# A new order for the front of a long fused kernel (results, scores, updates, x and loads), and a set place for three merges

## The chip, the core and the metric

The kernel runs on one core of one Trainium2 chip. The metric is device time in microseconds (us): the median of three runs of the kernel before is compared with that of the kernel after. A profile of one execution shows what each engine did: TensorE (PE, with its weight loads PEld), VectorE (DVE), ScalarE (ACT), GpSimd (POOL) and SyncE (SP), which issues nearly all the transfers (DMA).

## What is computed

The reference, cut to its core (float32 in and out; 2 sequences of 768 rows, 8 heads of 64, 512 dimensions):

```python
# 1. attention with decay, in blocks of 64 with a running state
intra = einsum('bhij,bhjd->bhid', einsum('bhic,bhjc->bhij', qb, kb) * Dmask, vb)
out   = intra + einsum('bhid,bhde->bhie', qb * lam_pow, kv_state)
kv_state = lam_block * kv_state + einsum('bhsd,bhse->bhde', kb * rev_pow, vb)
# 2. a token MLP and a channel MLP (1536 hidden)
h = relu(xt @ w_tok1) @ w_tok2        # xt = x transposed, 768 -> 256 -> 768
u = x + h.T
x = u + relu(u @ w_ch1) @ w_ch2
# 3. Fourier mixing, a norm, a channel MLP (2048 hidden)
u  = x + real(fft(fft(x, axis=1), axis=2))
un = (u - mean) / sqrt(var + 1e-6)
return u + relu(un @ m_ch1) @ m_ch2
```

## The kernel before

All products run on TensorE in float32r. Where float32 accuracy is wanted, each operand is a rounded part (hi) and the rest (lo), and `mm3` (L142 to L146) issues three matmuls. `split` (L136) makes the two parts of an activation: ScalarE writes hi, VectorE lo. Weights come from HBM as 8-byte words and go through a conveyor (`convert`, L291): a load by SyncE into one of three `raw` buffers, two ScalarE instructions (L233, L235), two VectorE **merges** of the words (L254, L255), then hi on ScalarE (L283) and lo on GpSimd (L284). A `raw` buffer is free for the next load when the merges have read it. Weights are named by their use: `t1` and `t2` of the token MLP, (a, 0, f) and (b, 0, f) of the first channel MLP, (a, 1, f) and (b, 1, f) of the second.

**Order of work.** TensorE and SyncE run in the order in which the program emits their instructions. The order on ScalarE, VectorE and GpSimd is made by a planner when the kernel is compiled; each engine then works through its list in order. `tc.issue_after(ins)` puts the instructions of its block behind `ins` in the list of the engine that they share.

**The front.** Attention has 8 steps n (2 sequences times 4 pairs of heads). The string `EARLY` gives the order as words: `l` loads a step (keys, queries, then keys and values; 384, 384 and 768 KB), `s` is scores (L410, then four VectorE multiplications L413), `u` is the update of the state (ScalarE first scales the keys, L432; L438; a chain of VectorE steps, L442 and L444), `r` is the result (L460 on scores, L466 on states; two ScalarE copies, L468). `x` transposes a half of one sequence and splits it (L483), `h` and `o` are the two products of the token MLP (`h00`: sequence 0, first half of the hidden units), `m` is one step of the channel MLP, `c` one turn of the conveyor, `d` the same without a load, `w` keeps TensorE busy with transposes, and `k` loads a constant. Loads 0 to 3 and the three of `t1` are issued before the string. A step's q, k, v lie in one of five `half` buffers, which the tiles of `x` and later ones use too.

**Later.** `run` takes the channel MLPs unit by unit; `WHEN` gives, for each of 25 Fourier and norm pieces of a sequence, the half step at which it is emitted. Piece 18 in the list was `fourier_columns(b, 2)` and piece 19 `norm(b, (0, 1, 2, 3))`. In `norm`, the VectorE instructions L950 write the normalized rows (`unf`), which TensorE transposes in `norm_out` (L959). The last part runs in units of seven products (`seven`), with three PSUM accumulators (pa, pb, pc) in two banks; VectorE reads them (L660 to L680) and so frees the banks.

Of the kernel before, what the change touches and what calls it, by code (L numbers as in the profile page):

```python
# [16 lines left out]
ALU = mybir.AluOpType  # L17
# [12 lines left out]
HS = S // 2  # L30
NQ = 256
# [2 lines left out]
BIG = 12 * NQ  # L34


EARLY = """s0 w u0 w s1 r0 u1 s2 u2 l4 r1 s3 u3 c r2 s4 l5 r3 u4 d d x00 s5 d l6 u5 r4 s6 x01 h00 c r5 c h01 l7 u6 s7 u7 r6 o00
r7 m o01 x10 m x11 m h10 m h11 m m o10 o11 k"""

WHEN = ((67, 71, 77, 73, 74, 77, 75, 77, 77, 79, 80, 81, 85, 83, 86, 85, 87, 84, 88, 90, 92, 91, 94, 97, 98),  # L40
        (92, 92, 93, 95, 97, 98, 100, 100, 103, 106, 106, 108, 108, 108, 112, 110, 113, 115, 116, 116, 119, 117,
         118, 120, 123))

# [19 lines left out]
def body(ctx: ExitStack, tc: tile.TileContext, qkv, kT, lam, w_tok1, w_tok2,  # L63
# [15 lines left out]
    tt = nc.vector.tensor_tensor  # L79
# [16 lines left out]
    on_act = {("table", 0): table_load}  # L96
    on_dve = {}

    chain = {("t1", 0): 3, ("t1", 1): 3, ("t1", 2): ("st", 5)}

# [116 lines left out]
    def stage_abs():  # L219

        if at_["abs"] >= at_["load"]:
            return
        job = jobs[at_["abs"]]
        kind, key = job
        at_["abs"] += 1
        if kind in ("single", "sums"):
            return
        m = raw_p.tile([P, 512], U32, tag="man", name="m_" + "_".join(map(str, key)), bufs=BUFS["man"])[:, :width(key)]
        mans[job] = m
        late = {("t1", 2): ("out", 2), ("b", 0, 1): ("out", 6), ("b", 0, 3): ("hid", 1), ("a", 0, 4): ("hid", 1)}  # L230
        with tc.issue_after(lag.get("act", on_act[late.get(key, ("keys", 3))])), behind_urgent():
            lo, hi = words(job)
            nc.scalar.activation(f32(m), f32(hi), AF.Copy, scale=DOWN)  # L233
            halves = raws[job].bitcast(U16)[:, :4 * width(key)].rearrange("p (n t) -> p n t", t=4)
            nc.scalar.activation(lo, halves[:, :, 1], AF.Identity, scale=2.0 ** -13, bias=floor_by)  # L235
# [187 lines left out]
    def attention_states(b, hp, dT, pw):  # L423

        n = f"{b}_{hp}"
        t, sts = pair[b, hp]
        kn, v = (t[:, i, :].rearrange("p (c j) -> p c j", j=C) for i in (1, 2))
        m = NP * b + hp
        behind = (("table", 0), ("keys", 0), ("out", 0), ("out", 1), ("out", 2), ("x", 0), ("out", m - 2))[min(m, 6)]
        with tc.issue_after(on_act[behind]):  # L430
            for a in range(2):
                on_act["keys", NP * b + hp] = nc.scalar.activation(  # L432
                    kn[:, :NC - 1, a * D:(a + 1) * D], kn[:, :NC - 1, a * D:(a + 1) * D], AF.Copy,
                    scale=dT[:, 2 * hp + a, C - 1:C]).ins
        ups = acc_bank(f"u_{n}")
        for c in range(NC - 1):
            for a in range(2):
                nc.tensor.matmul(ups[a * D:(a + 1) * D, c * D:(c + 1) * D], kn[:, c, a * D:(a + 1) * D],  # L438
                                 v[:, c, a * D:(a + 1) * D], start=True, stop=True)
        state = temp((NC - 1) * D, f"state_{n}").rearrange("p (c e) -> p c e", c=NC - 1)  # L440
        up = ups[:, :(NC - 1) * D].rearrange("p (c e) -> p c e", c=NC - 1)
        nc.vector.tensor_copy(state[:, 0], up[:, 0])  # L442
        for c in range(1, NC - 1):
            chained = stt(out=state[:, c], in0=state[:, c - 1], scalar=pw[:, hp, C - 1:C], in1=up[:, c],  # L444
                          op0=ALU.mult, op1=ALU.add).ins
        on_dve[NP * b + hp] = chained
        pair[b, hp] = t, sts, state
# [28 lines left out]
    def token_in(b, half):  # L476

        xt = half_tile([P, 3, 2, DM], f"x_{b}_{half}", F32R)
        for i in range(3):
            c = 3 * half + i  # L480
            px = (acc_bank if b == 0 else ph_bank if i == 2 else x_bank)(f"px_{b}_{c}")
            for hp in range(NP):
                nc.tensor.transpose(px[:, hp * P:(hp + 1) * P], xT[b][:, hp, c * P:(c + 1) * P], ident)  # L483
            with tc.issue_after(on_dve[4]) if b == half == 0 else ExitStack():
                split(px, xt[:, i, 0, :], xt[:, i, 1, :])
            xs[b, c] = xt[:, i]
        if b == half == 0:
            on_act["x", 0], on_dve["x", 0] = on_act["split"], on_dve["split"]

    def token_hidden(b, t):  # L490
        ps = (acc_bank, x_bank)[b](f"h1_{b}_{t}")
# [11 lines left out]
    def token_out(b, c):  # L503
        t = half_tile([P, 4, 2, HS], f"uh_{b}_{c}", F32R)
        uh[b, c] = t
        for dt in range(4):
            ps = (acc_bank, x_bank)[b](f"ht_{b}_{c}_{dt}")
            ds = slice(dt * P, (dt + 1) * P)
            for k in range(2):
                need(("t2", k, c))  # L510
                w = wt_tiles["t2", k, c]
                mm3(ps[:, :HS], (h1[b, k][0][:, ds], h1[b, k][1][:, ds]), (w[:, 0, :HS], w[:, 1, :HS]), k == 0, k == 1)
            u = xT[b][:, dt, c * HS:(c + 1) * HS]
            tt(out=u, in0=ps[:, :HS], in1=u, op=ALU.add)
            if dt:
                split(*todo_split)
            todo_split = u, t[:, dt, 0, :], t[:, dt, 1, :]
        split(*todo_split)
        if b == 1:
            live.difference_update([("t2", k, c) for k in range(2)])  # L520
# [117 lines left out]
    def hidden(n, src):  # L638
        t = hid_p.tile([P, 2, HS], F32R, tag="hid", name=n)
        relu_split(src, t[:, 0, :], t[:, 1, :])  # L640
        return t

    def seven(b, p, between):

        n = f"{b}_{p}"
        f = 2 * p
        for key in (("a", 1, f), ("a", 1, f + 1), ("s", 1, p)):
            need(key)
        wa, wb = wt_tiles["a", 1, f], wt_tiles["a", 1, f + 1]
        sums = {k: (wt_tiles["s", 1, p][i], 256 * j) for k, (i, j) in SUMS.items()}  # L650
        x0, x1 = unh[b, 0], unh[b, 1]
        ts_ = {j: tops[b, j] for j in range(1, 5)}
        pa = ph_bank(f"pa_{n}")
        product(pa, (wa, 0), x0[:, 0:2], True)
        m1 = temp(HS, f"m1_{n}")
        nc.scalar.activation(m1, pa[:, :HS], AF.Copy)
        pb = ph_bank(f"pb_{n}")
        product(pb, sums["S2"], ts_[2], True)
        u2 = temp(HS, f"u2_{n}")
        tt(out=u2, in0=pb[:, :HS], in1=m1, op=ALU.add)  # L660
        between()
        product(pa, (wa, 256), x0[:, 2:4], False)
        hid[1, b, 0, f] = hidden(f"hid_{n}_11", pa[:, :HS])
        if "next" in lag:
            lag["act"] = lag["next"]
        lag["next"] = urgent["act"]
        product(pb, sums["S3"], ts_[3], False)
        v3 = temp(HS, f"v3_{n}")
        tt(out=v3, in0=pb[:, :HS], in1=m1, op=ALU.add)
        between()  # L670
        pc = ph_bank(f"pc_{n}")
        product(pc, sums["S1"], ts_[1], True)
        tt(out=v3, in0=pc[:, :HS], in1=v3, op=ALU.add)
        hid[1, b, 1, f + 1] = hidden(f"hid_{n}_22", v3)
        product(pb, (wb, 256), ts_[4], False)
        tt(out=m1, in0=pb[:, :HS], in1=m1, op=ALU.add)
        hid[1, b, 0, f + 1] = hidden(f"hid_{n}_21", m1)
        between()
        product(pc, sums["S4"], x1[:, 2:4], False)
        tt(out=u2, in0=pc[:, :HS], in1=u2, op=ALU.add)  # L680
        hid[1, b, 1, f] = hidden(f"hid_{n}_12", u2)
        for key in (("a", 1, f), ("a", 1, f + 1), ("s", 1, p)):
            used(key)
        between()
# [188 lines left out]
    def fourier_columns(b, T):  # L873
# [24 lines left out]
        z = temp(2 * (NQ + 1), f"z_{b}_{T}")  # L898
        zs[b, T] = [z[:, i * (NQ + 1):(i + 1) * (NQ + 1)] for i in range(2)]
        for i, op in enumerate((ALU.subtract, ALU.add)):  # L900
            tt(out=sides(zs[b, T][i])[1], in0=at[:, :NQ].rearrange("p (h j) -> p h j", h=2),
               in1=ps[1][:, :NQ].rearrange("p (h j) -> p h j", h=2), op=op)
        ends = z.rearrange("p (i n) -> p i n", i=2)[:, :, 0:P + 1:P]
        nc.scalar.activation(ends, at[:, 0:NQ + 1:NQ].rearrange("p (o c) -> p o c", o=1).to_broadcast([P, 2, 2]),
                             AF.Copy)
# [22 lines left out]
    def norm(b, rows):  # L928
# [18 lines left out]
        convert(1, ops)  # L947
        for i, r in enumerate(rows):
            un = temp(DM, f"unf_{b}_{r}")
            ts(out=un, in0=u3[b][:, r, :], scalar1=mv[:, i, 0:1], scalar2=rs[:, i:i + 1],  # L950
               op0=ALU.subtract, op1=ALU.mult)
            uns[b, r] = un

    def norm_out(b, rows):
# [41 lines left out]
    for b in range(B):  # L996
        for h, (fn, *args) in zip(WHEN[b], (
# [1 line left out]
                (fourier_ab, b, 1, 0), (fourier_ab, b, 1, 1), (fourier_d, b, 1, 0), (fourier_d, b, 1, 1),  # L999
                (fourier_sums, b, 0), (fourier_sums, b, 1), (fourier_y, b, 0), (fourier_y, b, 1),  # L1000
                (fourier_gather, b), (fourier_columns, b, 0), (fourier_rows, b, 0), (fourier_columns, b, 1),
                (fourier_rows, b, 1), (fourier_mid, b), (fourier_columns, b, 2), (norm, b, (0, 1, 2, 3)),
                (fourier_rows, b, 2), (norm_out, b, (0, 1)), (norm_out, b, (2, 3)), (norm, b, (4, 5)),
                (norm_out, b, (4, 5)))):
            side.setdefault(h, []).append((fn, args))
# [207 lines left out]
```

## Time and profile before

| | before |
|---|---|
| median of 3 runs | 600.46 us (599.66 to 601.36) |
| the profiled execution's own time | 599.12 us |
| its span, first to last instruction | 597.3 us |
| TensorE busy | 584.4 us, 98% of the span |
| VectorE busy | 403.6 us, 68% |
| ScalarE busy | 264.4 us, 44% |
| GpSimd busy | 134.0 us, 22% |
| mean granted TensorE clock | 0.997 of full speed |

TensorE is busy nearly all the time, so a change to the order can only win what TensorE still waits. Its 12.9 us of idle time are the room there is, with a short stretch in which its clock was at half. Matmuls overlap in the profile and their ends are modelled, so an idle time in brackets is somewhat shorter than the delay in the starts.

### The profile page before, as it was taken

Reading aid. Unit: us, or ns where it says so; the run is one execution under the profiler, and the core shown is the slowest. Engines: PE = TensorE matmul, PEld = TensorE weight load, DVE = VectorE, ACT = ScalarE, POOL = GpSimd, SP = SyncE. Lnnn points to the kernel's source line nnn. Section 1 sums busy time; section 2 is a strip of 40 time slices with the busy share of each in tenths; the row PEclk is TensorE's granted clock in tenths of the full one; section 3 lists DMA queues with packets and bytes.
Section 4 is the critical chain, followed back from the end, with each engine's and each line's share of the span. In section 5 each row is a group of like instructions: output and inputs, shape, how many; then the busy total and the mean of one; then the engine's idle time right before and its main releaser. Section 6 shows DMA issues by size and latency. Waiting matters only on the chain.

```text
span 597.3 us, 9553 instructions
## 1 busy us (share of the span) xinstructions
PE 584.4 (98%) x3704; PEld 546.0 (91%) x3704; DVE 403.6 (68%) x765; ACT 264.4 (44%) x511; POOL 134.0 (22%) x114
## 2 busy tenths in 40 slices
PE   8899999999999999999999999999999999999997
PEld 7787899999999999999999999899889998899985
DVE  6787982565585656858787896867785864654435
ACT  1566871355565555535364451334433444331110
POOL 4254340022240051001452110014401223220000
PEclk9899999999999999999999999999999999999999
DMA  7975440033548756510232001002421232200005
GB/s 272 396 281 208 148 156 21 1 105 107 160 173 248 270 171 195 165 47 1 72 89 71 19 1 36 19 19 70 142 88 36 89 123 89 88 2 1 0 1 211
DMA packets 24637, 65.58 MB, mean 110 GB/s; under 512 B 2824, under 2 KB 3984, under 8 KB 24592
## 3 DMA queue, kind: packets, MB, share of 16 engines
q1 hardware_dynamic: 24304, 64.83, 32.5%
q8 instruction: 29, 0.48, 0.3%
q10 hardware_dynamic: 288, 0.14, 0.1%
q14 instruction: 16, 0.13, 0.1%
HBM read 54.99 MB, written 9.97 MB: 109 GB/s over the span
## 4 chain that ended last, share of the span: by engine, by line
PE 84%; DMA 6%; DVE 6%; ACT 2%; issue 1%; POOL 1%; SPq 0%; DVEq 0%; POOLq 0%; ACTq 0%
PE ac L145 12%; PE ac L146 12%; PE ac L144 12%; PE ph L144 8%; PE ph L146 8%; PE ph L145 8%; DMA qkv<-qkv 3%; DMA raw_t_0d<-w_tok 2%; PE pb L146 2%; PE pb L145 2%; PE pb L144 2%; PE pa L144 1%; PE pc L146 1%; PE pa L146 1%; PE pc L144 1%; PE pc L145 1%
## 5 line engine op out<-in xcount | busy, mean ns | idle before, releaser
L524 DVE SCALAR_TENSOR_TENSOR hid<-ph,hid 128x384 fp32r<-128x384 f32 x68 | 37.6, 554 | 60.5 <-ACT hid L523 60.5
L146 PE MATMUL ac<-w_b,hid 128*128 128x512 f32 x192 | 75.8, 395 | 0.0
L145 PE MATMUL ac<-w_b,hid 128*128 128x512 f32 x192 | 75.7, 394 | 0.0
L144 PE MATMUL ac<-w_b,hid 128*128 128x512 f32 x192 | 75.0, 391 | 0.0
L144 PE MATMUL ph<-uh,w_a 128*128 128x384 f32 x192 | 64.7, 337 | 0.0
L144 PE MATMUL ac<-hid,w_b 128*128 128x384 f32 x192 | 64.5, 336 | 0.0
L523 ACT ACTIVATE hid<-ph 128x384 fp32r<-128x384 f32 x68 | 33.1, 487 | 70.6 <-PE ph L146 70.3
L145 PE MATMUL ac<-hid,w_b 128*128 128x384 f32 x192 | 64.3, 335 | 0.0
L146 PE MATMUL ph<-uh,w_a 128*128 128x384 f32 x192 | 64.3, 335 | 0.0
L145 PE MATMUL ph<-uh,w_a 128*128 128x384 f32 x192 | 64.3, 335 | 0.0
L146 PE MATMUL ac<-hid,w_b 128*128 128x384 f32 x192 | 64.2, 335 | 0.0
L284 POOL TENSOR_TENSOR w_a<-m_a,w_a 128x512 fp32r<-128x512 f32 x18 | 25.6, 1422 | 131.4 <-ACT w_a L283 131.4
L146 PEld LDWEIGHTS ac<-w_b,hid 128*128 128x128 f32 x192 | 36.0, 188 | 7.7
L145 PEld LDWEIGHTS ac<-w_b,hid 128*128 128x128 f32 x192 | 36.1, 188 | 6.0
L144 PEld LDWEIGHTS ac<-w_b,hid 128*128 128x128 f32 x192 | 36.1, 188 | 5.8
L284 POOL TENSOR_TENSOR w_b<-m_b,w_b 128x512 fp32r<-128x512 f32 x18 | 26.0, 1445 | 46.5 <-ACT w_b L283 32.4
L144 PEld LDWEIGHTS ph<-uh,w_a 128*128 128x128 f32 x192 | 36.1, 188 | 0.2 <-ACT uh L138 0.2
L145 PEld LDWEIGHTS ac<-hid,w_b 128*128 128x128 f32 x192 | 36.1, 188 | 0.2 <-DVE hid L524 0.2
L145 PEld LDWEIGHTS ph<-uh,w_a 128*128 128x128 f32 x192 | 36.1, 188 | 0.1
L144 PEld LDWEIGHTS ac<-hid,w_b 128*128 128x128 f32 x192 | 36.1, 188 | 0.0
L146 PEld LDWEIGHTS ph<-uh,w_a 128*128 128x128 f32 x192 | 36.0, 188 | 0.0
L146 PEld LDWEIGHTS ac<-hid,w_b 128*128 128x128 f32 x192 | 36.0, 188 | 0.0
(504 smaller groups left out, 1429.1 us busy)
## 6 DMA issues: line engine op xcount, KB each, us to landing
qkv<-qkv SPq DMA_DIRECT2D x7, 768.0 KB, 10.1
single_scratch<-m_a SPq DMA_DIRECT2D x16, 256.0 KB, 4.3
qkv<-qkv SPq DMA_DIRECT2D x10, 384.0 KB, 6.1
kp<-kT SPq DMA_DIRECT2D x8, 384.0 KB, 6.9
out<-u SPq DMA_DIRECT2D x11, 256.0 KB, 2.0
single_scratch<-m_b SPq DMA_DIRECT2D x10, 256.0 KB, 5.3
raw_t_0d<-w_tok SPq DMA_DIRECT2D x2, 384.0 KB, 11.6
raw_t_1d<-w_tok SPq DMA_DIRECT2D x2, 384.0 KB, 3.0
```

The lines of the kernel that those rows point to most:

```text
L144: nc.tensor.matmul(ps, wt[0], xt[0], start=first, stop=False, **kw)
L145: nc.tensor.matmul(ps, wt[0], xt[1], start=False, stop=False, **kw)
L146: nc.tensor.matmul(ps, wt[1], xt[0], start=False, stop=last, **kw)
L284: nc.gpsimd.tensor_tensor(out=t[:, 1, :n], in0=src, in1=f32(t[:, 0, :n]), op=ALU.subtract)
L523: mark("act", nc.scalar.activation(hi, ps, AF.Relu))
L524: mark("dve", stt(out=lo, in0=ps, scalar=0.0, in1=f32(hi), op0=ALU.max, op1=ALU.subtract))
```

## The change

The front's words get another order: `r1` goes ahead of `u2`, `r3` ahead of `s4`, `r4` ahead of `u5`, `x01` ahead of `s6`, and the load of step 7 right behind that of step 6, ahead of the loads of `t2`. Some VectorE merges and ScalarE conversions of weights get another place behind which they are put: those of (t1, 2) behind the state of step 5 and the result of step 3, the conversion of (t2, 0, 0) behind the split of `x01`, the merges of (a, 0, 1) behind the second addition of `o00`, and those of (a, 1, 10) behind the end of the first unit of seven. In sequence 1 the norm is emitted ahead of the third columns, whose VectorE subtraction and addition go behind the second row of `unf`. For sequence 0 the two swapped times in `WHEN` keep the order as it was.

```diff
-EARLY = """s0 w u0 w s1 r0 u1 s2 u2 l4 r1 s3 u3 c r2 s4 l5 r3 u4 d d x00 s5 d l6 u5 r4 s6 x01 h00 c r5 c h01 l7 u6 s7 u7 r6 o00
+EARLY = """s0 w u0 w s1 r0 u1 s2 r1 u2 l4 s3 u3 c r2 l5 r3 s4 u4 d d x00 s5 l6 l7 r4 u5 d x01 s6 h00 c r5 c h01 u6 s7 u7 r6 o00
 r7 m o01 x10 m x11 m h10 m h11 m m o10 o11 k"""
-WHEN = ((67, 71, 77, 73, 74, 77, 75, 77, 77, 79, 80, 81, 85, 83, 86, 85, 87, 84, 88, 90, 92, 91, 94, 97, 98),
+WHEN = ((67, 71, 77, 73, 74, 77, 75, 77, 77, 79, 80, 81, 85, 83, 86, 85, 87, 84, 90, 88, 92, 91, 94, 97, 98),
...
-    chain = {("t1", 0): 3, ("t1", 1): 3, ("t1", 2): ("st", 5)}
+    chain = {("a", 1, 10): "unit", ("t1", 0): 3, ("t1", 1): 3, ("t1", 2): 5, ("a", 0, 1): ("ht", 1)}
...
-        late = {("t1", 2): ("out", 2), ("b", 0, 1): ("out", 6), ("b", 0, 3): ("hid", 1), ("a", 0, 4): ("hid", 1)}
+        late = {("t1", 2): ("out", 3), ("t2", 0, 0): ("x", 1), ("b", 0, 1): ("out", 6), ("b", 0, 3): ("hid", 1), ("a", 0, 4): ("hid", 1)}
...
-        behind = (("table", 0), ("keys", 0), ("out", 0), ("out", 1), ("out", 2), ("x", 0), ("out", m - 2))[min(m, 6)]
+        behind = (("table", 0), ("keys", 0), ("out", 0), ("out", 1), ("out", 3), ("x", 0), ("out", m - 2))[min(m, 6)]
...
-        if b == half == 0:
-            on_act["x", 0], on_dve["x", 0] = on_act["split"], on_dve["split"]
+        if b == 0:
+            on_act["x", half] = on_act["split"]
...
-            tt(out=u, in0=ps[:, :HS], in1=u, op=ALU.add)
+            added = tt(out=u, in0=ps[:, :HS], in1=u, op=ALU.add).ins
+            if b == c == 0:
+                on_dve["ht", dt] = added
...
         hid[1, b, 1, f] = hidden(f"hid_{n}_12", u2)
+        on_dve.setdefault("unit", urgent["dve"])
...
-            tt(out=sides(zs[b, T][i])[1], in0=at[:, :NQ].rearrange("p (h j) -> p h j", h=2),
-               in1=ps[1][:, :NQ].rearrange("p (h j) -> p h j", h=2), op=op)
+            with tc.issue_after(on_dve["unf", b, 1]) if (b, T) == (1, 2) else ExitStack():
+                tt(out=sides(zs[b, T][i])[1], in0=at[:, :NQ].rearrange("p (h j) -> p h j", h=2),
+                   in1=ps[1][:, :NQ].rearrange("p (h j) -> p h j", h=2), op=op)
...
-            ts(out=un, in0=u3[b][:, r, :], scalar1=mv[:, i, 0:1], scalar2=rs[:, i:i + 1],
-               op0=ALU.subtract, op1=ALU.mult)
+            on_dve["unf", b, r] = ts(out=un, in0=u3[b][:, r, :], scalar1=mv[:, i, 0:1], scalar2=rs[:, i:i + 1],
+                                     op0=ALU.subtract, op1=ALU.mult).ins
...
-                (fourier_rows, b, 1), (fourier_mid, b), (fourier_columns, b, 2), (norm, b, (0, 1, 2, 3)),
+                (fourier_rows, b, 1), (fourier_mid, b), (norm, b, (0, 1, 2, 3)), (fourier_columns, b, 2),
```

## Rows read from the trace of the kernel before

**Rows 1.** Windows: busy us (and count) of PE, PEld, DVE, ACT, POOL; clock; DMA.
```profile
0.00:72.00 72.00, 65.20 (x827) 56.30 (x828) 55.66 (x140) 41.20 (x80) 30.02 (x37) 0.98 0.73 269
72.00:140.00 68.00, 68.00 (x389) 66.45 (x389) 41.22 (x72) 32.19 (x61) 14.00 (x9) 1.00 0.22 71
```
**Rows 2.** Timeline of TensorE, 0 to 72: start, duration, instruction, [idle before <-releaser].
```profile
30.34 1.61 PE L410 MATMUL s<-qkv,kp 64*128 64x128 f32 x24 [1.12 <-DMA qkv<-qkv]
31.88 1.53 PE L460 MATMUL po<-st,qkv 128*64 128x128 f32 x24
...
34.58 0.80 PE L438 MATMUL u<-qkv 128*64 128x64 f32 x20
...
48.11 0.51 PE L145 MATMUL h<-x,w_t 128*128 128x512 f32 x1 [0.70 <-DVE x L139]
...
60.02 1.19 PE L438 MATMUL u<-qkv 128*64 128x64 f32 x19 [0.49 <-ACT qkv L432]
...
66.88 0.34 PE L146 MATMUL ht<-w_t,h1s 128*128 128x384 f32 x1
67.84 0.45 PE L144 MATMUL ht<-w_t,h1s 128*128 128x384 f32 x1 [0.63 <-DVE xT L514]
```
**Rows 3.** Waits of TensorE, whole span: total us, times, longest.
```profile
PE pc L144 <- DVE v L673: 0.6, 1, 0.6
PE pn L959 <- DVE unf L950: 0.5, 1, 0.5
PE pa L144 <- DVE m L676: 0.4, 1, 0.4
```
**Rows 4.** Windows of 1 and 5 us in the front, columns as in rows 1.
```profile
19.00:20.00 1.00, 0.91 (x9) 0.61 (x6) 0.98 (x2) 0.60 (x2) 0.08 (x1) 0.50 1.00 326
```
**Rows 5.** Timeline of ScalarE, 32 to 36.
```profile
32.14 1.02 ACT L432 ACTIVATE qkv<-qkv,att 128x320 f32<-128x320 f32 x2 [2.38 <-DMA qkv<-qkv]
...
35.32 0.84 ACT L468 ACTIVATE xT<-po 128x384 f32<-128x384 f32 x2
```
**Rows 6.** The chain that ended last, front: start, duration, what.
```profile
30.72 11.56 DMA raw_t_0d<-w_tok
...
52.58 6.80 DMA qkv<-qkv
```
**Rows 7.** Windows, columns as in rows 1.
```profile
30.00:35.00 5.00, 4.66 (x82) 4.23 (x84) 4.46 (x7) 2.86 (x6) 2.49 (x2) 1.00 1.02 406
...
70.00:75.00 5.00, 5.00 (x50) 4.66 (x47) 5.00 (x11) 4.19 (x9) 1.13 (x1) 1.00 0.17 34
```
**Rows 8.** Timeline of VectorE, 40 to 50.
```profile
40.55 1.19 DVE L254 SCALAR_TENSOR_TENSOR m_t<-m_t,raw_t_2d 128x512 uint32<-128x512 uint32 x1
...
45.52 1.94 DVE L413 TENSOR_TENSOR st<-s,att 128x512 f32<-128x512 f32 x4
47.38 1.87 DVE L139 TENSOR_TENSOR x<-px,x 128x512 fp32r<-128x512 f32 x3
```
**Rows 9.** Timeline of VectorE around the norm of sequence 1.
```profile
370.22 0.16 DVE L946 SCALAR_TENSOR_TENSOR rs<-t,rs 128x4 f32<-128x4 f32 x1
...
373.07 0.75 DVE L901 TENSOR_TENSOR z<-at,pm 128x256 f32<-128x256 f32 x2 [0.43 <-PE pm L146]
373.74 2.96 DVE L950 TENSOR_SCALAR unf<-u,mv,rs 128x512 f32<-128x512 f32 x4
```
**Rows 10.** Timeline of VectorE in the first unit of seven.
```profile
425.06 0.69 DVE L254 SCALAR_TENSOR_TENSOR m_a<-m_a,raw_a_10d 128x512 uint32<-128x512 uint32 x1 [1.32 <-ACT raw_a_10d L235]
425.67 0.55 DVE L673 TENSOR_TENSOR v<-pc,v 128x384 f32<-128x384 f32 x1
426.14 1.36 DVE L255 SCALAR_TENSOR_TENSOR m_a<-raw_a_10d,m_a 128x512 uint32<-128x512 uint32 x1
427.43 0.54 DVE L676 TENSOR_TENSOR m<-pb,m 128x384 f32<-128x384 f32 x1
```
**Rows 11.** Timeline of GpSimd in the same unit.
```profile
425.68 1.27 POOL L284 TENSOR_TENSOR w_b<-raw_b_9s,w_b 128x512 fp32r<-128x512 f32 x1 [1.05 <-issue]
```

## The prediction, as it was put on record

> **What bounds the kernel.** I read the page first (busy shares, the 40 slices), then the windows by stage, then TensorE's waits and its timeline at each wait, and last the lists of the engines that ended them. The windows show that the room lies in two places. In the first 72 us TensorE works 65.20, in the next 68 us all 68.00 [rows 1]; from there on it is the bound, and its only waits are short ones. So the end moves with TensorE's starts: a delay that is taken out of the front moves everything behind it, as long as the other engines follow. VectorE works 55.66 of the first 72 us [rows 1] and is full in 70 to 75 [rows 7]; it is the one that may not follow.
>
> The timeline gives four waits in the front that the new order touches: 1.12 before the scores of step 4 (a load), 0.70 in the token product (the split of `x01`), 0.49 before the update of step 7 (its keys, a load), 0.63 in `o00` (VectorE's addition) [rows 2]. Behind the front there are three more: 0.5 before the transposes of the norm, 0.6 and 0.4 in the first unit of seven [rows 3].
>
> **A bracket is less than the delay.** In `o00` the start moves from 66.88 to 67.84, 0.96, where the matmul ahead lasts 0.34 and its bracket says 0.63 [rows 2]. The matmuls overlap by about half in this stream, so the regular step is about 0.17 (an estimate, half of 0.34) and the delay 0.79; the first matmul after it takes 0.45 in place of 0.34. Together 0.9, that is 0.27 above the bracket. I add 0.27 to each wait as an estimate.
>
> **The front, part by part.** No instruction is added or removed on TensorE; all terms are waits.
>
> *`r3` ahead of `s4`.* The scores of step 4 waited for their load until 30.34. A result takes 31.88 to 34.58, 2.70, and scores 30.34 to 31.88, 1.54 [rows 2]. With `r3` in the gap, the result starts at about 29.22 (30.34 less 1.12), ends at 31.9, and the scores end at 33.5. The wait of 1.12 is gone. What comes next is `u4`: its keys could be scaled from 32.14, when their load was there [rows 5], and are now put behind the copies of `r3`. Those take 0.84 in the worst case from 31.9, so until 32.7, and the scaling 1.02 [rows 5]: ready at 33.8, 0.3 after `u4` could start at 33.5. I count 1.12 + 0.27 - 0.3 = 1.1.
>
> *`r1` ahead of `u2`.* This part runs at half clock: the granted clock is 0.50 in 19 to 20 [rows 4], the 1.2 GHz level, in a stretch in which TensorE stood for 0.09 of 1.00. All that comes ahead of `r1` is as before, so the dip stays. What it saves is at most the piece that TensorE idled in that window, 0.09 [rows 4]; I count 0, and the work of the dip is only another.
>
> *`x01` ahead of `s6`.* VectorE made four multiplications of scores first (45.52, 1.94) and then the splits of `x01` (47.38, 1.87) [rows 8], and the product waited at 48.11 [rows 2]. With `x01` emitted ahead of the scores, its splits come ahead of them: 1.94 earlier, more than the wait of 0.70. I count 0.70 + 0.27 = 1.0. What is late next is (t1, 2): its merge stood at 40.55 [rows 8], between scores and state of step 5, and is now put behind that state. With u5 later than `r4` but the whole 1.1 earlier, I put that state's end near 42.3; two merges of about 0.65, ScalarE's rounding (some 0.6) and GpSimd's part (1.27, rows 11) bring it to 45.5. The product wants it for its fifth block, some 0.5 after the place of the old wait, which is 48.11 less 0.70 less 1.12 = 46.3: 46.8. It fits by 1.3 (estimates throughout).
>
> *Load 7 early.* SyncE is moved past the loads of `t2` here. The old last transfer of load 7 started at 52.58 and took 6.80 [rows 6], so its keys ended at 59.4 and `u7` waited 0.49 [rows 2]. Issued behind load 6 it needs the buffer of step 3, free with `r3` at 31.9, and lands near 45, 10 us ahead of `u7`. I count 0.49 + 0.27 = 0.8. Its price: 384 + 384 + 768 KB go ahead of the first `t2` load, at 406 GB/s [rows 7] 3.9 us. That load was issued at 30.72 and landed at 42.28 [rows 6]; now near 46.2. The work that hides it: `t2` is first used in `o00`, which ran around 66.88 [rows 2] and will run near 63. Its conversion, put behind the split of `x01` (44 to 45), loses little.
>
> *The merges of (a, 0, 1)* leave `o00`'s additions free: 0.63 + 0.27 = 0.9. Their cover: the next units of the first MLP, which TensorE takes behind `o00`, a result and half of `o01`.
>
> Sum of the front: 1.1 + 1.0 + 0.8 + 0.9 = 3.8. The lower bound is 0, if all of it is lost again (below nothing only by the last rival); the upper 4.1, without the 0.3 of `u4`. I take 2.9. The reason: from about 65 to 85 VectorE is full (5.00 in 70 to 75, rows 7), with splits, additions and merges in one list, so TensorE arriving 3.8 earlier should wait there for part of it; a quarter is my estimate.
>
> **The norm of sequence 1.** The scale was ready at 370.22 + 0.16, but VectorE's list had the columns' two instructions ahead of `unf`, and these waited for TensorE until 373.07 [rows 9]; `unf` started at 373.74, 0.74 a row. With `unf` rows 0 and 1 ahead they end before 373.0 even behind another unit's instruction, and the transposes that waited at about 375 find them. I count 0.5 + 0.27 = 0.7. The columns' pair comes at most 1.5 later, and the third rows that need it come units later.
>
> **The first unit.** The first merge waits on VectorE 1.32 for ScalarE, and `v` (L673) stands behind it; the second merge, 1.36 long, holds `m` (L676) back to 427.43 [rows 10]. With both merges behind the unit's end, `v` and `m` run when their sums are there. I count 0.6 + 0.4 + 2 x 0.27 = 1.5, less 0.3, since the bank that `u` (L680) frees comes next: 1.2. Bounds 0.4 and 1.5. Queued behind the merges are SyncE's store of the slab and the loads behind it; the next use is several units away.
>
> The second merge lasted 1.36 where the first, of the same size, took 0.69, and it lay beside a GpSimd instruction, 425.68 to 426.95 [rows 10, 11]. The Trainium skill, SBUF — State Buffer, section "Who interferes with whom", says that a VectorE instruction with two SBUF inputs and a GpSimd one that reads SBUF exclude each other, and the later is blocked for the whole of the other; the trace agrees, since 426.95 plus about 0.55 is the merge's end. GpSimd's own part of the moved slab then lies in the second unit, which is a rival below.
>
> **Sum.** 2.9 + 0.7 + 1.2 = 4.8. The profiled execution took 599.12 (span 597.3 and 1.8 around it), so 594.3; it lies 1.3 under the median of 600.46. From the median: **595.6**.
>
> **Rivals.**
>
> *VectorE takes the front back* (0.20). TensorE comes earlier to `o01` and the first units, but the additions and splits there come when VectorE's list gets to them, and that list is full [rows 7]. For: no gap in 70 to 75. Against: it idles some 16 us in the first 72 [rows 1], and merges can wait. Front 0.2, later parts 1.9: 600.46 - 2.1 = 598.4.
>
> *GpSimd's part of (a, 1, 10) holds the second unit* (0.10). It takes about 1.3 and stood beside the end of the first unit; in the second it can hold a VectorE instruction by the 0.67 that it cost the merge (1.36 less 0.69). Against: that unit has gaps. Time 595.6 + 0.7 = 596.3.
>
> *The planner moves the waits* (0.08). `issue_after` only sets one order; the rest of the three lists is made anew, and new waits of the same size could open. Nothing in the trace can rule it out. Time 600.4, no change.
>
> *Slower: the token product starves* (0.08). The conversion of `t2` waits in ScalarE's list for a load that is now late, and the rounding of (t1, 2) stands behind it. The product then has its fifth block 3.1 after the landing (conversion 1.2, rounding 0.6, GpSimd 1.27; estimates). With 46.2 that is 49.3 against 46.8: 2.5 lost, and still faster. It ends over 0.3% slower if the loss passes 3.8 + 1.9 + 1.8 = 7.5, a landing after 51.2, 5 us beyond mine; a fall of the clock to half, as at 19 [rows 4], would make it 1.7 sooner. Then near 602.5.
>
> **How the numbers follow.** The forecast has 0.54, the rivals 0.20, 0.10, 0.08 and 0.08. About 0.3% (1.8 us) is what a measurement here can tell from none. Faster: 0.54, 0.10 and 0.12 of VectorE's 0.20 (2.1 us lies near the line): 0.76. Same: 0.08 of that, the planner's 0.08: 0.16. Slower: 0.08. The range goes from all terms in full (4.1 + 0.7 + 1.5 = 6.3, and 0.5 for the scatter of the runs: 593.7) up to 599.2, which takes in VectorE's case and leaves the last two out.
>
> **What would show it.** Right: no wait over 0.3 ahead of scores 4, `u7`, in `h00` or `o00`; the first unit of the channel MLP starts some 3 us earlier than before; the norm's and the first unit's waits on VectorE gone. Wrong: a wait for `w_t` in `h00`, gaps of TensorE in 68 to 90, a second stretch at half clock, or the old waits at other names after 300 us.

## The result, and the profile after

The changed kernel takes 595.03 us (594.03 to 595.71, 6 runs) against 600.49 (599.66 to 601.36, 6 runs): a ratio of 0.9908, interval 0.9893 to 0.9923, 5.5 us less. 595.6 was forecast, in 593.7 to 599.2. Measured again beside other kernels (run 9), the ratio was 0.9923, 0.9903 to 0.9942.

The profiled execution took 594.03, span 592.2. The starts of the same matmuls in the two timelines of TensorE cut the span into stages:

| stage, by TensorE's starts | before | after | less |
|---|---|---|---|
| to the first unit of the channel MLP | 71.79 | 68.75 | 3.04 |
| from there to the norm's transposes (sequence 1) | 303.69 | 303.01 | 0.68 |
| to the first unit of seven | 41.21 | 41.17 | 0.04 |
| two units of seven | 27.13 | 25.78 | 1.35 |
| from there to the end | 153.5 | 153.5 | 0.0 |
| span | 597.3 | 592.2 | 5.1 |

The rows of TensorE's timeline behind the table (start, duration, instruction, [idle before <-releaser]): the first unit of the channel MLP, the norm's transposes, the first and the third unit of seven. Before:

```profile
71.79 0.45 PE L144 MATMUL ph<-uh,w_a 128*128 128x384 f32 x1
...
375.48 1.08 PE L959 MATMUL pn<-ident,unf 128*128 128x128 f32 x8 [0.45 <-DVE unf L950]
...
416.69 0.33 PE L144 MATMUL pa<-un,w_a 128*128 128x384 f32 x1
...
443.82 0.33 PE L144 MATMUL pa<-un,w_a 128*128 128x384 f32 x1
```

After:

```profile
68.75 0.44 PE L144 MATMUL ph<-uh,w_a 128*128 128x384 f32 x1
...
371.76 1.03 PE L963 MATMUL pn<-ident,unf 128*128 128x128 f32 x8
...
412.93 0.33 PE L144 MATMUL pa<-un,w_a 128*128 128x384 f32 x1
...
438.71 0.33 PE L144 MATMUL pa<-un,w_a 128*128 128x384 f32 x1
```

Each column comes from one execution, and the first stage scatters most: runs 2 and 3 below have the front of before and start the channel MLP at 73.08 and 74.55, and run 9 is the changed kernel again and starts it at 69.66.

The transposes of the norm no longer carry a wait [rows 3]. The waits of TensorE that are left, whole span (total, times, longest):

```profile
PE u L438 <- ACT qkv L432: 2.4, 2, 1.7
PE warm L1059 <- POOL ident masks.py:199: 1.4, 1, 1.4
PE pq L144 <- DVE u L927: 0.6, 1, 0.6
PE s L410 <- DMA qkv<-qkv: 0.5, 1, 0.5
PE po L466 <- DVE state L444: 0.4, 1, 0.4
PE h L146 <- POOL w_t L284: 0.3, 1, 0.3
PE pc L144 <- DVE hid L526: 0.2, 1, 0.2
```

The waits for VectorE in the norm and in the unit's `v` and `m` are gone from the list. In the front the four old waits [rows 2] are gone too, but others stand in their place. TensorE's timeline, 14 to 62, after:

```profile
16.66 1.25 PE L438 MATMUL u<-qkv 128*64 128x64 f32 x20 [1.72 <-ACT qkv L432]
17.91 1.61 PE L410 MATMUL s<-qkv,kp 64*128 64x128 f32 x24
...
22.88 1.61 PE L410 MATMUL s<-qkv,kp 64*128 64x128 f32 x24
25.15 1.19 PE L438 MATMUL u<-qkv 128*64 128x64 f32 x19 [0.67 <-ACT qkv L432]
...
31.58 1.61 PE L410 MATMUL s<-qkv,kp 64*128 64x128 f32 x24
33.12 0.93 PE L438 MATMUL u<-qkv 128*64 128x64 f32 x20
...
47.27 0.50 PE L146 MATMUL h<-x,w_t 128*128 128x512 f32 x1 [0.35 <-POOL w_t L284]
...
57.68 0.80 PE L438 MATMUL u<-qkv 128*64 128x64 f32 x20
...
60.96 0.75 PE L466 MATMUL po<-qkv,state 64*64 64x128 f32 x8 [0.37 <-DVE state L444]
```

The update of step 3 at 25.15 waits for its keys, the product at 47.27 for GpSimd's part of (t1, 2), and the result of step 6 at 60.96 for a state. The scores of step 4 (31.58) and the updates of steps 4 and 7 (33.12, 57.68) no longer wait. Behind 68 us TensorE does not stand at all (windows: busy us and count of PE, PEld, DVE, ACT, POOL; clock; DMA):

```profile
68.00:140.00 72.00, 72.00 (x422) 70.23 (x419) 45.89 (x77) 36.13 (x68) 15.69 (x11) 1.00 0.25 82
```

VectorE in the norm, after: `unf` follows the scale at once, and the columns' pair comes behind it [rows 9]; four rows take 1.92, where they took 2.96.

```profile
367.12 0.17 DVE L950 SCALAR_TENSOR_TENSOR rs<-t,rs 128x4 f32<-128x4 f32 x1
367.32 1.92 DVE L954 TENSOR_SCALAR unf<-u,mv,rs 128x512 f32<-128x512 f32 x4
369.15 0.55 DVE L526 SCALAR_TENSOR_TENSOR hid<-ph,hid 128x384 fp32r<-128x384 f32 x1
369.96 0.76 DVE L905 TENSOR_TENSOR z<-at,pm 128x256 f32<-128x256 f32 x2 [0.26 <-PE pm L146]
```

VectorE in the first unit of seven, after: `v` and `m` run as soon as their sums are there (the brackets name TensorE), and the two merges lie at 424.95 and 426.48, behind the unit [rows 10].

```profile
420.94 0.56 DVE L675 TENSOR_TENSOR v<-pc,v 128x384 f32<-128x384 f32 x1 [0.95 <-PE pc L146]
421.98 0.56 DVE L678 TENSOR_TENSOR m<-pb,m 128x384 f32<-128x384 f32 x1 [0.49 <-PE pb L146]
422.46 0.95 DVE L526 SCALAR_TENSOR_TENSOR hid<-v,hid 128x384 fp32r<-128x384 f32 x1
...
424.95 0.68 DVE L254 SCALAR_TENSOR_TENSOR m_a<-m_a,raw_a_10d 128x512 uint32<-128x512 uint32 x1
...
426.48 0.69 DVE L255 SCALAR_TENSOR_TENSOR m_a<-raw_a_10d,m_a 128x512 uint32<-128x512 uint32 x1
```

### The profile page after: what moved, and what is told of

Same layout as the page of the kernel before. It is cut to its first block, busy times and chain, and to the rows that moved or that the text cites. A ratio compares the mean times of both kernels' runs of the same rounds, so it can differ in the third digit from the quotient of the medians.

```text
span 592.2 us, 9551 instructions
## 1 busy us (share of the span) xinstructions
PE 582.3 (98%) x3704; PEld 545.1 (92%) x3704; DVE 401.7 (68%) x765; ACT 265.3 (45%) x511; POOL 131.7 (22%) x114
## 4 chain that ended last, share of the span: by engine, by line
PE 89%; DVE 5%; DMA 4%; ACT 1%; SPq 1%; issue 1%; DVEq 0%; ACTq 0%
PE ac L145 13%; PE ac L146 13%; PE ac L144 13%; PE ph L144 8%; PE ph L146 8%; PE ph L145 8%; PE pb L144 2%; PE pb L145 2%; PE pb L146 2%; DMA qkv<-qkv 2%; PE pc L144 1%; PE pa L146 1%; PE pc L146 1%; PE pa L144 1%; PE pc L145 1%; PE pa L145 1%
```

## The experiments

Twelve kernels, in three groups of four on one chip each; each ratio is to the kernel before, run beside them (medians 600.01, 600.08 and 599.82). The stage lengths come from TensorE's starts, as in the table above.

**1. The front alone** (the changed kernel without the norm's and the first unit's edits).

```diff
-    chain = {("a", 1, 10): "unit", ("t1", 0): 3, ("t1", 1): 3, ("t1", 2): 5, ("a", 0, 1): ("ht", 1)}
+    chain = {("t1", 0): 3, ("t1", 1): 3, ("t1", 2): 5, ("a", 0, 1): ("ht", 1)}
...
-                (fourier_rows, b, 1), (fourier_mid, b), (norm, b, (0, 1, 2, 3)), (fourier_columns, b, 2),
+                (fourier_rows, b, 1), (fourier_mid, b), (fourier_columns, b, 2), (norm, b, (0, 1, 2, 3)),
```

> The front alone: the new order, its places for conversions and merges; the norm and the merges of (a, 1, 10) as before. Theory (three parts that add up): ratio 0.995, some 3.0 us less than before, with the first unit of the channel MLP 3.0 earlier and the three waits behind 300 us as before. Rival (the parts hang together, VectorE's list downstream is what the front shifts): less than 2 us, with other waits behind 68 us. Rival (the clock): the gain is about 1.5 us in executions that show the stretch at half clock and about 3 in those that do not.

Measured 597.36, ratio 0.9963 (0.9944 to 0.9981): 2.7 us less. The old waits of the norm (0.45) and of the unit (0.79 for `m`) are there, and two units of seven take 26.93. The first unit of the channel MLP starts at 70.42, 1.4 earlier than in the profile of before. That is less than 3.0 above all because the update of step 3 waits 2.24 for its keys. The first rival falls: from 68 us on TensorE is busy 72.00 of 72. The rival of the clock is not settled by this run. So the parts can be taken apart, and the front's size depends on when loads land.

**2. The norm alone**, on the kernel before (the swap in the list and in `WHEN`, and the columns' pair behind `unf`).

```diff
-                (fourier_rows, b, 1), (fourier_mid, b), (fourier_columns, b, 2), (norm, b, (0, 1, 2, 3)),
+                (fourier_rows, b, 1), (fourier_mid, b), (norm, b, (0, 1, 2, 3)), (fourier_columns, b, 2),
...
+            with tc.issue_after(on_dve["unf", b, 1]) if (b, T) == (1, 2) else ExitStack():
```

> The norm alone, on the kernel before. Theory: the wait of 0.45 before the norm's transposes is gone and no other comes; 0.7 us less, ratio 0.9988. Rival (the parts hang together): within 0.2 us of before, since the columns' pair is later and holds the third rows.

Measured 599.90, ratio 0.9996 (0.9981 to 1.0011). The wait before the transposes is gone, but the stage that holds the norm is only 0.16 shorter (303.53 against 303.69; with the norm as before, runs 1, 3 and 4 have 303.48 to 303.57), since another wait came 11 us earlier, before a transpose of the rows:

```profile
365.49 0.77 PE L916 MATMUL pu<-ident,xT 128*128 128x128 f32 x4 [0.32 <-DVE u L924]
```

The theory was half wrong: the edit removes its wait, but in this list of VectorE another takes its place. In the changed kernel it does not (303.01, and 302.95 in run 9). The rival's reason, the later pair, is not it either: the new wait lies ahead of that pair.

**3. The first unit alone**, on the kernel before.

```diff
-    chain = {("t1", 0): 3, ("t1", 1): 3, ("t1", 2): ("st", 5)}
+    chain = {("a", 1, 10): "unit", ("t1", 0): 3, ("t1", 1): 3, ("t1", 2): ("st", 5)}
...
+        on_dve.setdefault("unit", urgent["dve"])
```

> The merges of (a, 1, 10) behind the first unit of seven alone, on the kernel before. Theory: the waits of 0.57 and 0.43 in that unit are gone, 1.2 to 1.4 us less, ratio 0.9978. Rival (GpSimd's part of the moved slab holds the second unit): 0.7 us less, with a new wait in the second unit.

Measured 599.07, ratio 0.9986 (0.9970 to 1.0002). The time alone does not tell it from no change, but the stage does: two units of seven take 25.78 in place of 27.13, 1.35 less, the same as in the changed kernel, and without a new wait in the second unit. In the three other profiles with the old merges (runs 1, 2 and 4) the two units take 26.93 or 26.94, so the edit is worth 1.15 to 1.35. The theory holds; the rival falls.

**4. Load 7 early, alone**, on the kernel before.

```diff
-... u4 d d x00 s5 d l6 u5 r4 s6 x01 h00 c r5 c h01 l7 u6 s7 u7 r6 o00
+... u4 d d x00 s5 d l6 l7 u5 r4 s6 x01 h00 c r5 c h01 u6 s7 u7 r6 o00
```

> The load of step 7 moved behind that of step 6, alone, on the kernel before. Theory (the transfers ahead of t2 are hidden): the wait of 0.49 before the update of step 7 is gone, t2's first load lands near 46 in place of 42.3 and nobody waits for it; 0.8 us less, ratio 0.9987. Rival (the token product starves): the conversion of t2 holds ScalarE's list, a wait of 1 us or more in the token product, and the time is 0.5 to 2 us over before.

Measured 601.71, ratio 1.0023 (1.0006 to 1.0039): slower. Both theories missed the place. The waits before the update of step 7, in the token product and in `o00` are gone. In their place the result of step 6 stands four times, 2.3 us in all, for its states:

```profile
61.94 0.43 PE L466 MATMUL po<-qkv,state 64*64 64x128 f32 x4 [0.35 <-DVE state L444]
63.70 0.44 PE L466 MATMUL po<-qkv,state 64*64 64x128 f32 x4 [1.33 <-DVE state L444]
64.49 0.69 PE L466 MATMUL po<-qkv,state 64*64 64x128 f32 x4 [0.36 <-DVE state L444]
```

VectorE's list in the same stretch of this kernel shows why: a merge of (a, 0, 1), 1.65 long, stands between two states. GpSimd's part of another slab lies beside it, from 61.65 to 62.91.

```profile
61.62 0.27 DVE L444 SCALAR_TENSOR_TENSOR state<-state,att,u 128x64 f32<-128x64 f32 x1
61.81 1.65 DVE L254 SCALAR_TENSOR_TENSOR m_a<-m_a,raw_a_1d 128x512 uint32<-128x512 uint32 x1
63.38 0.27 DVE L444 SCALAR_TENSOR_TENSOR state<-state,att,u 128x64 f32<-128x64 f32 x1
```

And while TensorE ran in such pieces, its granted clock fell: 0.57 in 64 to 68 (of the two levels, 1.2 and 2.4 GHz, mostly the lower), where the kernel before had none.

```profile
64.00:68.00 4.00, 3.64 (x17) 3.18 (x14) 3.24 (x11) 3.72 (x7) 1.28 (x1) 0.57 0.41 131
```

**5. Load 7 back**, in the changed kernel.

```diff
-... u4 d d x00 s5 l6 l7 r4 u5 d x01 s6 h00 c r5 c h01 u6 s7 ...
+... u4 d d x00 s5 l6 r4 u5 d x01 s6 h00 c r5 c h01 l7 u6 s7 ...
```

> The changed kernel with the load of step 7 back behind the second token product. Theory (the early load is worth the wait before the update of step 7): that wait returns with 0.5 to 1.1 us, and the time is 0.8 us over that of the changed kernel, ratio to before about 0.992. Rival (as in the run with load 7 alone, the early load is a loss by itself): the waits in the last results' state part go, and the time is 0.5 us or more under that of the changed kernel, ratio 0.990 or less.

Measured 597.23, ratio 0.9952 (0.9938 to 0.9967). The waits for this load return, and there are two, for the scores of step 7 and for its update:

```profile
58.60 1.61 PE L410 MATMUL s<-qkv,kp 64*128 64x128 f32 x24 [1.19 <-DMA qkv<-qkv]
61.00 1.19 PE L438 MATMUL u<-qkv 128*64 128x64 f32 x19 [0.79 <-ACT qkv L432]
```

Within the new order the early load thus takes out 2.0 of waits, where 0.8 was forecast. It is worth less than that: the result of step 6 does not wait for states here, and in the changed kernel it does (0.37, and 0.73 in run 9). From the update of step 6 to the first unit this run takes 15.2, the changed kernel 13.3 and in run 9 14.1, so 1.1 to 1.9 is left. The changed kernel did not run in this group; by the ratios of the other two it is 1.7 to 2.6 us faster than this one. Alone the early load cost 1.7. So its sign depends on the other edits.

**6. The merges of (t1, 2) behind the scores again**, in the changed kernel.

```diff
-("t1", 2): 5,
+("t1", 2): ("st", 5),
```

> The changed kernel with the merges of (t1, 2) put behind the scores of step 5 again. Theory (behind the state they come too late and cost the wait of 0.35 for GpSimd's part in the token product): that wait is gone and the product starts its last block earlier, 0.3 to 0.6 us less than the changed kernel, ratio to before about 0.990. Rival (the merges hold the state and the splits of x01): a wait of over 0.5 us for x or for the state, and 0.5 us more than the changed kernel.

Measured 598.03, ratio 0.9970 (0.9948 to 0.9993). The wait of 0.35 in the product is gone, but `o00` waits 1.8 for a ScalarE copy and the result of step 6 0.60 for a VectorE split. The theory fell: the place costs 0.35 where it is, and the lists behind it are worse with the other one. Not all of the loss need be the edit's: the update of step 4 also waits 1.42 for its keys, and a transpose ahead of the norm 0.73 for VectorE.

**7. The merges of (a, 0, 1) free again**, in the changed kernel.

```diff
-("t1", 2): 5, ("a", 0, 1): ("ht", 1)}
+("t1", 2): 5}
```

> The changed kernel with the merges of (a, 0, 1) free again. Theory (they held the additions of the first token output): the wait of 0.6 in that product returns, 0.9 us more than the changed kernel, ratio to before about 0.992. Rival (the other moves had already freed the additions): the same time as the changed kernel within 0.3 us, and no wait there.

Measured 596.26, ratio 0.9939 (0.9919 to 0.9958), and no wait in `o00`. The rival is right that the additions were free already: the old 0.63 is gone in run 4 (load 7 early alone) too. It is also gone in run 5, where load 7 is late and the merges have their place. So with either of the two edits there is no such wait, and no run tells which of them takes it out in the changed kernel. Whether this edit saves anything, the times do not tell. The profile shows a loss without it in another place: the stage from the first unit to the norm takes 304.20 (303.01 and 302.95 in the changed kernel), with three waits of 0.26 to 0.28, two of them for VectorE at 83.61 and 211.28.

**8. TensorE kept busy ahead of the update of step 1**, in the changed kernel (eight extra transposes, not used).

```diff
-... s1 r0 u1 s2 r1 ...
+... s1 r0 w u1 s2 r1 ...
```

> The changed kernel with eight idle transposes ahead of the update of step 1, where TensorE waits for the keys; the transposes are extra and their result is not used. Theory (the executions that are about 1.5 us longer are those with the stretch at half clock, which the waits at 15 to 18 us bring about): no such stretch, and the median is 0.5 to 0.9 us under that of the changed kernel, with less scatter. Rival (the scatter comes from the landing of loads alone): the same median within 0.3 us, or 0.3 us more where the keys are there early.

Measured 596.61, ratio 0.9942 (0.9923 to 0.9961), no better. The clock stays at 1.00 in 18 to 22, but the scores of step 2 then wait 1.58 for a state and the update of step 3 0.86 for its keys. The theory fell as to the gain: what TensorE gains there, it waits at the next state and the next load. It also fell as to the clock: three of the six executions still have a mean granted clock of 0.996 or 0.997. They took 597.05 on average and the others 596.04, so the executions with the lower clock are indeed the longer ones.

**9. The changed kernel again**, beside the next three.

> [...] Expected: ratio to before 0.991 to 0.994, a wait for keys before the update of step 3 of 0.5 to 2.4 us, and no wait in the norm or for VectorE in the first unit's second half.

Measured 594.97, ratio 0.9923 (0.9903 to 0.9942). Here it is the update of step 4 that waits, 1.03, and step 3 does not; the first unit of the channel MLP starts at 69.66, two units of seven take 25.78, the stage with the norm 302.95. I had named the wrong step for the wait.

**10. `r1` behind `u2` again**, in the changed kernel.

```diff
-... s1 r0 u1 s2 r1 u2 l4 s3 u3 ...
+... s1 r0 u1 s2 u2 l4 r1 s3 u3 ...
```

> The changed kernel with the result of step 1 behind the update of step 2 again. Theory (r1 ahead of u2 saves nothing and uncovers the update of step 3, whose keys land late): the wait before that update is under 0.3 us, and the time is 0.5 to 2 us under that of the changed kernel in this group. Rival (r1 covers the update of step 2): a wait of 0.5 us or more returns before the update of step 2, or a stretch at half clock, and the time is the same as that of the changed kernel within 0.5 us or more.

Measured 595.24, ratio 0.9927 (0.9911 to 0.9943), the same as run 9. No wait for keys before the updates of steps 3 and 4, but the stretch at half clock is there:

```profile
18.00:22.00 4.00, 3.92 (x51) 3.46 (x50) 2.89 (x9) 1.01 (x2) 1.25 (x2) 0.57 1.03 407
```

So this edit is worth nothing that the times could tell, as forecast, and in the two profiles the stretch at half clock is nearly made up: the first unit starts at 69.83 against 69.66 in run 9.

**11. `r2` ahead of `u3`**, in the changed kernel, as cover for the late keys.

```diff
-... u2 l4 s3 u3 c r2 l5 r3 s4 ...
+... u2 l4 s3 r2 u3 c l5 r3 s4 ...
```

> The changed kernel with the result of step 2 ahead of the update of step 3, a result of 2.7 us as cover for the late keys. Theory (the landing of the keys of step 3 is the front's next bound): the wait before that update is gone, and the time is 0.7 to 2 us under that of the changed kernel in this group. Rival (the next load is late as well): the wait moves to the scores or the update of step 4 with the same size, and the time is the same within 0.5 us.

Measured 595.47, ratio 0.9926 (0.9909 to 0.9943). The wait moves to the update of step 4, at 0.26, and the first unit starts at 69.24, 0.4 earlier than in run 9. But a new wait of 0.64 for VectorE opens at 210 us, so nothing is won.

**12. The same, and the merges of (b, 0, 0) behind the state of step 6.**

```diff
-("a", 0, 1): ("ht", 1)}
+("a", 0, 1): ("ht", 1), ("b", 0, 0): 6}
```

> As the run with the result of step 2 ahead of the update of step 3, and with the merges of (b, 0, 0) put behind the state of step 6, where the changed kernel waits 0.37 us before the last part of the result of step 6. Theory (VectorE's list between states and merges makes that wait): it is gone, and the time is 0.4 to 0.6 us under that of the run without. Rival (the additions of the first token output come later instead): the same within 0.3 us, with a wait in that product.

Measured 595.76, ratio 0.9929 (0.9912 to 0.9947). The wait for the state is gone and `o00` waits 0.69 for a ScalarE copy: the rival's wait in that product, for another engine. The update of step 4 waits 1.84 here, so the two lists cannot be compared by it alone. None of the versions beats the changed kernel; runs 9 to 12 cannot be told apart by their times.

## Why the prediction was right

**The sum.** 4.8 was forecast, 5.1 measured between the two profiles and 5.5 between the medians. Stage by stage the two profiles give 3.04 for the front (2.9 forecast), 0.68 for the norm (0.7) and 1.35 for the first unit (1.2). The last two are borne out by other profiles within 0.2: 0.5 to 0.7 and 1.15 to 1.35. Run 1 shows the front alone at 2.7 by its medians. That the front came within 0.14 is luck in part, since profiles of the same front differ by up to 2.8 at that point, and its terms did not come as forecast:

| TensorE's start of | before | after | lead | gained since the row above | forecast |
|---|---|---|---|---|---|
| scores of step 3 | 24.31 | 22.88 | 1.43 | 1.43 | 0 (`r1`) |
| update of step 4 | 34.58 | 33.12 | 1.46 | 0.03 | 1.1 (`r3`) |
| second token product | 52.88 | 51.09 | 1.79 | 0.33 | 1.0 (`x01`) |
| `o00` | 63.75 | 61.64 | 2.11 | 0.32 | 0.8 (load 7) |
| first unit of the channel MLP | 71.79 | 68.75 | 3.04 | 0.93 | 0.9 (a, 0, 1) |

**A bracket understates its delay.** In the norm the step from the matmul ahead into the transposes is 0.84 before (374.64 to 375.48) and 0.23 after (371.53 to 371.76). The bracket said 0.45 and the delay was 0.61, with 0.04 more in the transposes: 0.20 above the bracket, where I had put 0.27.

**`r3` ahead of `s4`, and `r1` ahead of `u2`.** The wait of 1.12 before the scores of step 4 is gone, and the update of step 4 starts at 33.12 where it did at 34.58 [rows 2]; I had 33.8 at the latest. By the table this lead is not `r3`'s: it is there at the scores of step 3. Run 10 shows `r3` nearly by itself, since it has `r1` in the old place and the stretch at half clock, as before. Its scores of step 3 start at 24.41 (24.31 before) and its update of step 4 at 33.48, 1.10 earlier than before. So the step was right in its mechanism, 1.1 as forecast in this one pair, and short of one rival: what is late next is another load. With `r1` ahead, the keys of step 3 land too late for its update. Its wait was 0.67 in the profile after, 2.24, 2.40 and 1.81 in runs 1, 5 and 7, and in run 9 the update of step 4 waited 1.03 instead.

The profiles of before and after also differ in the clock: 6.70 from the scores of step 2 to those of step 3 before, with the stretch at half clock, and 4.97 after, without it. I had counted that the dip stays. It did not in this execution, nor in run 9, and it did in run 10. So the 1.43 came with a change of the clock that I had not forecast, and the late update of step 3 took the 1.1 that I had: it starts 2.27 after the scores of its step, where it was 1.54 before (24.31 to 25.85), and the result behind it starts 0.98 later, where it was 0.63 (25.85 to 26.48). One reading is that up to 33 us the landing of loads sets the pace, and what TensorE gains or loses ahead of it is waited out. Run 10 against run 9 fits it; the times of all executions do not fit it in full. In 13 of the 14 sets of runs of one kernel in one group that have both kinds, the executions with a mean granted clock of 0.997 or less are on average longer than the others, by 1.3 us over all sets; the span at half clock before was worth about as much, 1.73. For the kernel before it is 0.3 to 1.7. Whether the clock makes them longer, or the late load that TensorE stood for ahead of it, stays open.

**`x01` ahead of `s6`.** The wait for the split (0.70) is gone; of the 1.0 only 0.33 came, since (t1, 2) did not fit by 1.3, as I had put it, but missed by 0.35 (0.4 to 0.6 in the runs on the changed kernel that show that wait). I had taken two merges of 0.65 behind a state that ends near 42.3, though the row that I read it from has the first merge at 1.19 [rows 8]. VectorE's list after has the state's end at 42.75, a first merge of 1.31 and one of the splits of `x01` between the two merges. Against the forecast they cost 0.45, 0.66 and 0.60:

```profile
42.48 0.27 DVE L444 SCALAR_TENSOR_TENSOR state<-state,att,u 128x64 f32<-128x64 f32 x1
42.67 1.31 DVE L254 SCALAR_TENSOR_TENSOR m_t<-m_t,raw_t_2d 128x512 uint32<-128x512 uint32 x1
43.90 0.68 DVE L139 TENSOR_TENSOR x<-px,x 128x512 fp32r<-128x512 f32 x1
44.50 0.68 DVE L255 SCALAR_TENSOR_TENSOR m_t<-raw_t_2d,m_t 128x512 uint32<-128x512 uint32 x1
```

The first merge lies beside an instruction of GpSimd that ends at 43.43, and itself ends 0.55 later, as the merge of the first unit did in the prediction (timeline of GpSimd, after):

```profile
41.88 1.55 POOL L418 TENSOR_TENSOR qkv<-qkv,att 128x640 f32<-128x640 f32 x1 [2.02 <-DMA qkv<-qkv]
```

**Load 7.** The transfers ahead of `t2` are hidden, as forecast: the first `t2` load was issued at 34.17, converted from 45.75, and nobody waited for it. The wait that it takes out was put too small: 2.0 in run 5, where 0.8 was counted. Of that the waits of the result of step 6 take a part back, so the lead grew by 0.32 between the profiles and by 1.1 to 1.9 against run 5. And it is no separate term: alone it lost 1.7 (run 4), through merges between states, a wait that none of my rivals named.

**(a, 0, 1).** 0.9 was counted for it, and the lead grows by 0.93 there. But run 7 shows no wait in its absence, and run 4, with the early load alone, none either. I had counted as this edit's a wait that the early load can take out as well.

**VectorE taking a quarter back.** It did not: TensorE is busy 72.00 of the 72 us from 68 on, in the profile after and in run 9. I had called VectorE full from about 65 to 85, which the windows of before do not show:

```profile
75.00:80.00 5.00, 5.00 (x35) 4.96 (x34) 3.70 (x6) 3.37 (x6) 4.20 (x3) 1.00 0.78 281
```

The loss that I had put there was made in the front itself, by the keys, by (t1, 2) and by the state of step 6. So the front's 2.9 is right in size and wrong in its reason, and the lead that the other terms did not bring came in the stretch where the clock had changed.

**The rivals.** GpSimd's part of the moved slab lay at 427.91 in the second unit and held nothing there. The token product did not starve for `t2`. The planner's case is the one that the experiments kept meeting, in runs 2, 4, 6, 11 and 12: each edit removes its wait, and VectorE's or ScalarE's new list opens another. The changed kernel is a set of edits that fit together, and I had given that case too little.

## What to carry to other kernels

Cut the span at the starts of the same instructions on the engine that bounds it: the stage of the first unit showed 1.15 to 1.35 us where medians of the whole could not. Take several profiles before trusting a stage length to better than 0.2 us, and more in a stage that waits for loads. When an edit takes out one wait in lists that a planner makes, look for the next wait in every stage, since the same edit gave a gain in one set of edits and a loss in another (load 7: 1.1 to 1.9 by its stage, and minus 1.7). A load that lands late can take back the gains ahead of it, so price what comes after the landing first.

## What was not expected of the hardware

The four rows of `unf` took 2.96 us before and 1.92 after, the same instructions and shapes. Before, the first of them took 1.59 and the others some 0.53 (the rows of `unf`: shortest, median and longest in ns, first and last start):

```profile
L950 DVE TENSOR_SCALAR unf<-u,mv,rs x4: 532/534/1592, 373.7 to 376.2; 128x512 f32<-128x512 f32 x4
```

GpSimd had begun beside the first, at 373.76 (timeline of GpSimd, before):

```profile
373.76 1.28 POOL L284 TENSOR_TENSOR w_a<-raw_a_7s,w_a 128x512 fp32r<-128x512 f32 x1 [15.20 <-issue]
```

After, the same GpSimd instruction starts at 370.65, when the rows are done. The profiles of runs 1, 3 and 4, which keep the old norm, show the same meeting with the same 1.59. I had put the whole delay down to the columns' pair, and read the 2.96 as 0.74 a row. At 0.53 each, the two rows that the transposes take first would have ended near 374.7 even behind the columns' pair, and TensorE was ready for them near 374.9 (an estimate from these rows). So the meeting by itself may account for the whole wait, and moving `unf` ahead took it out; no run moves GpSimd's part alone. The Trainium skill, SBUF — State Buffer, section "Who interferes with whom", says that a VectorE instruction of this kind can use the port pair that it shares with GpSimd, and that the one that comes second is blocked until the first ends. The trace agrees that the two exclude each other: the long row ends about 0.3 after GpSimd's end at 375.04. It does not show the order that the page gives: the row started 0.02 ahead of GpSimd's instruction and was the one delayed.

The granted clock did not fall at 18 to 22 us in all executions of the same order of work. It was 0.57 before and in runs 2 and 3, and 1.00 in run 4, whose words are the same up to there; TensorE had waited 1.00 and 1.03 ahead of the update of step 1 in the profiles of before and of run 4. It was 1.00 in both profiles of the changed kernel, though TensorE had waited 1.72 there in one and 0.24 in the other, and 0.57 with `r1` back.
